# A scheduling edge between the down matmuls of one unit and the gate of the next

## The chip, the core and the metric

The kernel runs on one core of one Trainium2 chip. Its time is the device time of one execution in microseconds (us), and the median of three runs of the kernel before is 2629.54 us (2627.05 to 2629.81). Engines are named as in the profile: PE is the matmul engine, PEld its weight loads, ACT the activation engine, DVE the vector engine, POOL the general-purpose engine, SP the queue that issues the DMAs.

## What is computed

A batch of 8 sequences of 3008 rows with 256 features goes through a spectral layer (a real FFT along the sequence, a complex 256x256 product with a bias, soft thresholding at 0.01, the inverse FFT) and then, row by row, through a feed-forward layer:

```python
X = np.fft.rfft(x, axis=1)
Yr = Xr @ w_r - Xi @ w_i + b_r
Yi = Xr @ w_i + Xi @ w_r + b_i
Yr = np.sign(Yr) * np.maximum(np.abs(Yr) - lam, 0.0)      # Yi the same
y = np.fft.irfft(Y, n=x.shape[1], axis=1)
...
h = x @ w_in                       # 256 -> 2048
g = h * np.clip(h + 3.0, 0.0, 6.0) / 6.0
return (g @ w_out).astype(np.float32)     # 2048 -> 256
```

The change touches only the order of the feed-forward part.

## The kernel before

The 24064 rows are cut into 47 chunks of 512. The hidden width of 2048 is cut into 8 bands of 256, so there are 47 x 8 = 376 **units**, a chunk and a band each. A unit has three parts.

**The up product** (`block`, through the helper at L137) is 7 **groups** of three matmuls, 256 columns wide, a Strassen-like scheme on high and low parts of the numbers. Their numbers are the `n` of `block(i, n, ...)`. One PSUM tile `pb` collects groups 1, 6, 7 and 4 one upon the other, and after each of them ACT copies the sum out (`p1`, `u2`, `u3` at L585, and the last one straight into `h` at L619) before the next group may add to it. The next group can't begin before that copy has been read out. The same holds when the tile changes hands: `pb` has two buffers, so group 1 of unit i+2 waits for the `h` copy after group 4 of unit i. I call the four places (1 to 6, 6 to 7, 7 to 4, and 4 to group 1 of unit i+2) the **hand-overs** of `pb`. A tile `pc` with one buffer takes groups 5 and 3, a tile `pd` with one buffer group 2; DVE adds them to the copies (L590) and so fills `h`.

**The gate** (`gate`) is four operations in a row on the whole unit, 128x1024: `r = relu(h + 3)` on ACT (L626), `r = min(r, 6) * h` on DVE (L628), the high part `gs` by a cast on ACT (L130), the low part `gs` by a subtraction on DVE (L131). ACT and DVE carry out their instructions strictly in the order of the program.

**The down product** (`down`) is 12 matmuls of 512 columns (L649) into two PSUM tiles `po`: eight that need the high part of `gs` and four that need its low part. After the eighth band of a chunk `po` is scaled (`ot`) and stored.

The spectral layer of the later sequences is laid between the units: `fill` calls its generators by a table of slots. It brings matmuls into `ps_a`, copies, casts and DMAs, and it comes to an end before the units do, so that the last units stand almost alone.

The Python code only gives the instructions and their data. The order on each engine is made by a list scheduler, which walks a modelled timeline: of the instructions whose inputs are there it takes the one that comes first in the code, and `tc.high_priority()` lifts the copies and adds of the up product. So the down matmuls of a unit go wherever the model has both parts of `gs` ready and PE free. In the code, `gate(i-1)` begins in pass i of the loop and `down(i-3, step)` is spread over the same pass; the code's order therefore already has the first operation of gate i+1 ahead of the downs of unit i.

Of the kernel before, what the change touches and what calls it, by code (L numbers as in the profile page):

```python
# [13 lines left out]
AF = mybir.ActivationFunctionType  # L14
# [86 lines left out]
def spectral_ffn(ctx: ExitStack, tc: tile.TileContext, x, w_r, w_i, bias, w_in, w_out, f47, f64, g64, sgn, out):  # L101
    nc = tc.nc
# [11 lines left out]
    def space(shape, dt, name, tag=None):  # L114
        tag = tag or name
        return sb.tile(shape, dt, name=name, tag=tag, bufs=depth.get(tag, 1))
# [11 lines left out]
    def split(hi, lo, src, on=None):  # L128

        nc.scalar.copy(out=hi, in_=src)  # L130
        (on or nc.vector).tensor_tensor(out=lo, in0=src, in1=hi.bitcast(F32), op=ALU.subtract)  # L131
# [14 lines left out]
    def loaded(src, rows, cols, name, at=None):  # L146

        hi = const.tile([rows, cols], F32R, name=name + "_hi")
        lo = const.tile([rows, cols], F32R, name=name + "_lo")
        st = const.tile([rows, cols], F32, name=name + "_all") if at is None else at  # L150
        nc.sync.dma_start(out=st[:rows, :cols], in_=src)
        return hi, lo, st[:rows, :cols]
# [5 lines left out]
    nf = NFT // 2  # L158
    three = const.tile([P, 1], F32, name="three")
# [192 lines left out]
    with tc.issue_after(stores[-1].ins):  # L352
        r, k = [loaded(w, P, 2 * D, n, t) for w, n, t in ((w_r, "w_r", spare[7]), (w_i, "w_i", spare[8]))]
# [219 lines left out]
            yield  # L573

    units = [(c, f) for c in range(NC) for f in range(nf)]
    hs, ps_of, keep, gs, pos = {}, {}, {}, {}, {}

    def block(i, n, ps, start):
        c, f = units[i]
# [42 lines left out]
    def gate(i):  # L622

        h = hs.pop(i)
        r = space([P, 2, T], F32, "r")
        nc.scalar.activation(out=r, in_=h, func=AF.Relu, bias=three, scale=1.0)  # L626
        yield
        nc.vector.scalar_tensor_tensor(out=r, in0=r, scalar=6.0, in1=h, op0=ALU.min, op1=ALU.mult)  # L628
        t = gs[i] = space([P, 2, 2, T], F32R, "gs")
        split(t[:, 0], t[:, 1], r)  # L630
        yield
# [6 lines left out]
    )  # L638

    def down(i, step):  # L640

        c, f = units[i]
        g = gs[i]
        for u, dh, which, low in STEPS[step]:
            if f == 0 and step < 2 and u == 0 and which == "l":
                pos[dh] = ps_o.tile([P, 512], F32, name=f"po{dh}")
            ft = 2 * f + u
            w = wout_s["hl".index(which)]
            nc.tensor.matmul(  # L649
                out=pos[dh],  # L650
                lhsT=w[:, ft * D + dh * P : ft * D + (dh + 1) * P],
                rhs=g[:, low, u],
                start=f == 0 and u == 0 and which == "l",
                stop=f == nf - 1 and u == 1 and low == 1,
            )
            if f == nf - 1 and u == 1 and low == 1:
                ot = space([P, T], F32, "ot")
                if dh:
                    nc.vector.tensor_scalar(out=ot, in0=pos[dh], scalar1=1.0 / 6.0, scalar2=None, op0=ALU.mult)
                else:  # L660
                    nc.scalar.mul(out=ot, in_=pos[dh], mul=1.0 / 6.0)
                nc.sync.dma_start(out=out[dh * P : (dh + 1) * P, c * T : (c + 1) * T], in_=ot)
# [68 lines left out]
    for i in range(n + 3):  # L731
        for kind, f in ((in_band, i), (out_band, i - 3)):
            while 0 <= f < nf and (kind, f) not in ready:
                turn(LATE)
        if i < n:
            phase_a(i)
        gated(i - 2)
        fill(4 * i)
        if 0 <= i - 3 < n:
            down(i - 3, 0)  # L740
        if 0 <= i - 1 < n:
            phase_c(i - 1)
        fill(4 * i + 1)
        if 0 <= i - 3 < n:
            down(i - 3, 1)
        if i < n:
            phase_b(i)
        fill(4 * i + 2)
        if 0 <= i - 3 < n:
            down(i - 3, 2)  # L750
        if 0 <= i - 1 < n:
            phase_d(i - 1)
            gates[i - 1] = gate(i - 1)
            gated(i - 1)
        fill(4 * i + 3)
        if 0 <= i - 3 < n:
            down(i - 3, 3)
            gs.pop(i - 3)
# [47 lines left out]
```

## Time and profile before

| | |
|---|---|
| median of three runs | 2629.54 us |
| the profiled execution | 2630.53 us |
| its span, first to last instruction | 2628.8 us |
| PE busy | 2554.0 us (97%), 16392 matmuls |
| DVE busy | 1967.7 us (75%) |
| ACT busy | 1816.7 us (69%) |
| POOL busy | 762.9 us (29%) |
| mean granted clock of the matmul engine | 0.993 |
| unit 16 begins | 263.2 us |
| unit 325 begins | 2338.2 us |

Times in the rows are us from the first instruction, and a row's second number is how long the instruction (or the merged run of xN of them) took. Matmuls overlap in the records: one of 256 columns is listed with 0.28 us, yet the next starts 0.115 us later. What PE does is therefore read from starts, not from lengths. A bracket `[0.46 <-ACT p L585]` says that the engine was idle for 0.46 us before that instruction, and what released it.

### The profile page before, as it was taken

How to read it: one execution, taken by the hardware profiler on the slowest of the kernel's cores; microseconds unless marked ns; L12 is line 12 of the kernel's file. 1: busy time of each engine (PE TensorE's matmuls, PEld its weight loads, DVE VectorE, ACT ScalarE, POOL GpSimd, SP SyncE). 2: the span in 40 equal slices, each digit the busy share in tenths (PEclk: the TensorE clock that was granted, in tenths of full speed). 3: DMA queues.
4: the chain of work that ended last, by engine and by line, in shares of the span. 5: the costliest groups of instructions: out<-in, count | busy, mean ns of one | idle time of the engine just before them, and what ended most of it. 6: DMA issues, size and time to landing. Idle time of an engine off the chain costs nothing.

```text
span 2628.8 us, 44438 instructions
## 1 busy us (share of the span) xinstructions
PE 2554.0 (97%) x16392; PEld 2278.1 (87%) x16392; DVE 1967.7 (75%) x3195; ACT 1816.7 (69%) x3578; POOL 762.9 (29%) x726
## 2 busy tenths in 40 slices
PE   5789999999999999999999999999999999999999
PEld 4568989988898988998898888898989889888887
DVE  7777877777777777777778777787777777666766
ACT  5467776767677676676766677766776766776666
POOL 3223333333323332333314243233321121131310
PEclk8999999999999999999999999999999999999999
DMA  8643422232123212322223222222222111110000
GB/s 245 204 127 91 121 83 79 82 89 69 56 85 90 76 58 64 86 86 82 62 66 91 75 65 74 74 81 80 66 76 64 44 60 50 40 31 25 12 17 17
DMA packets 150081, 199.97 MB, mean 76 GB/s; under 512 B 16847, under 2 KB 103943, under 8 KB 149863
## 3 DMA queue, kind: packets, MB, share of 16 engines
q1 hardware_dynamic: 149863, 197.13, 25.7%
q8 instruction: 129, 2.11, 0.4%
q14 instruction: 89, 0.73, 0.1%
HBM read 97.45 MB, written 74.97 MB: 66 GB/s over the span
## 4 chain that ended last, share of the span: by engine, by line
PE 83%; DVE 6%; ACT 5%; DMA 4%; issue 1%; SPq 0%; POOL 0%; ACTq 0%; DVEq 0%
PE po L649 37%; PE pb L137 17%; PE ps_a L137 10%; PE pc L137 9%; PE pd L137 4%; PE ps_a L523 3%; PE ps_a L394 2%; ACT r L626 2%; DVE r L628 1%; ACT gs L130 1%; DMA scr<-a 1%; DMA xin<-in_x 1%; DVE gs L131 1%; DVE h L590 1%; DMA zt<-tc 1%
## 5 line engine op out<-in xcount | busy, mean ns | idle before, releaser
L649 PE MATMUL po<-gs,w_out_hi 128*128 128x512 f32 x3008 | 1008.5, 396 | 0.0
L628 DVE SCALAR_TENSOR_TENSOR r<-r,h 128x1024 f32<-128x1024 f32 x376 | 485.2, 1290 | 253.0 <-ACT r L626 250.9
L649 PEld LDWEIGHTS po<-gs,w_out_hi 128*128 128x128 f32 x3008 | 540.6, 188 | 83.7
L649 PE MATMUL po<-gs,w_out_lo 128*128 128x512 f32 x1504 | 602.9, 401 | 5.3 <-ACT gs L130 3.2
L137 PE MATMUL pb<-yb,w_in_hi 128*128 128x256 f32 x3008 | 570.1, 279 | 0.0
L626 ACT ACTIVATE r<-h,three 128x1024 f32<-128x1024 f32 x376 | 435.6, 1158 | 193.8 <-DVE h L590 191.1
L131 DVE TENSOR_TENSOR gs<-r,gs 128x1024 fp32r<-128x1024 f32 x376 | 481.9, 1282 | 75.6 <-ACT gs L130 74.1
L137 PEld LDWEIGHTS pb<-yb,w_in_hi 128*128 128x128 f32 x3008 | 459.1, 188 | 18.2
L130 ACT CAST gs<-r 128x1024 fp32r<-128x1024 f32 x376 | 396.7, 1055 | 97.3 <-DVE r L628 94.5
L590 DVE TENSOR_TENSOR h<-pc,u 128x256 f32<-128x256 f32 x752 | 315.3, 419 | 183.7 <-PE pc L137 168.4
L131 POOL TENSOR_TENSOR yb<-T,yb 128x256 fp32r<-128x256 f32 x184 | 176.7, 966 | 908.5 <-ACT yb L130 905.3
L137 PE MATMUL pb<-yb,w_in_lo 128*128 128x256 f32 x1504 | 430.5, 287 | 3.8 <-ACT p L585 0.9
L585 ACT COPY u<-pb 128x256 f32<-128x256 f32 x752 | 279.4, 374 | 112.6 <-PE pb L137 93.8
L649 PEld LDWEIGHTS po<-gs,w_out_lo 128*128 128x128 f32 x1504 | 282.7, 188 | 63.8 <-ACT gs L130 14.3
L137 PEld LDWEIGHTS pb<-yb,w_in_lo 128*128 128x128 f32 x1504 | 282.6, 188 | 28.2 <-ACT h L619 4.0
L137 PE MATMUL pc<-yb,w_in_hi 128*128 128x256 f32 x1504 | 296.8, 279 | 0.0
L137 PEld LDWEIGHTS pc<-yb,w_in_hi 128*128 128x128 f32 x1504 | 229.8, 188 | 11.7
L137 PE MATMUL pc<-yb,w_in_lo 128*128 128x256 f32 x752 | 217.7, 289 | 2.0 <-DVE h L590 1.7
L585 ACT COPY p<-pb 128x256 f32<-128x256 f32 x376 | 140.3, 374 | 71.6 <-PE pb L137 70.5
L619 ACT COPY h<-pb 128x256 f32<-128x256 f32 x376 | 141.2, 376 | 53.0 <-PE pb L137 51.7
L590 DVE TENSOR_TENSOR h<-pd,p 128x256 f32<-128x256 f32 x376 | 157.0, 418 | 19.8 <-ACT p L585 13.5
L137 PEld LDWEIGHTS pc<-yb,w_in_lo 128*128 128x128 f32 x752 | 141.6, 188 | 16.4 <-DVE h L590 3.9
(139 smaller groups left out, 3873.7 us busy)
## 6 DMA issues: line engine op xcount, KB each, us to landing
bt<-scr SPq DMA_DIRECT2D x96, 256.0 KB, 3.0
scr<-pt SPq DMA_DIRECT2D x96, 256.0 KB, 2.3
zt<-tc SPq DMA_DIRECT2D x376, 64.0 KB, 2.0
out<-ot SPq DMA_DIRECT2D x94, 256.0 KB, 2.3
scr<-a SPq DMA_DIRECT2D x96, 240.0 KB, 2.6
qt<-scr SPq DMA_DIRECT2D x96, 240.0 KB, 3.5
xin<-in_x SPq DMA_DIRECT2D x42, 480.0 KB, 4.6
f<-in_f SPq DMA_DIRECT2D x96, 128.0 KB, 2.7
```

The costliest lines, as they stand in the source:

```text
L130: nc.scalar.copy(out=hi, in_=src)
L131: (on or nc.vector).tensor_tensor(out=lo, in0=src, in1=hi.bitcast(F32), op=ALU.subtract)
L137: nc.tensor.matmul(out=ps, lhsT=a, rhs=b, start=start and n == 0, stop=stop and n == len(todo) - 1, skip_group_check=more,)
L394: nc.tensor.matmul(out=psv[:, dh, :, u, :], lhsT=data[:, u, dh * P : (dh + 1) * P], rhs=f[:, u, :], start=True, stop=True,)
L523: nc.tensor.matmul(out=ps[:, cs * w + g * rows : cs * w + (g + 1) * rows], lhsT=qt[:rows, cs, g, dh * P : (dh + 1) * P], rhs=f47_s[2][:row ...
L585: nc.scalar.copy(out=t, in_=ps)
L590: nc.vector.tensor_tensor(out=to, in0=ps, in1=keep.pop((i, n)), op=ALU.add)
L619: nc.scalar.copy(out=hs[i][:, 1, :H], in_=pb)
L626: nc.scalar.activation(out=r, in_=h, func=AF.Relu, bias=three, scale=1.0)
L628: nc.vector.scalar_tensor_tensor(out=r, in0=r, scalar=6.0, in1=h, op0=ALU.min, op1=ALU.mult)
L649: nc.tensor.matmul(out=pos[dh], lhsT=w[:, ft * D + dh * P : ft * D + (dh + 1) * P], rhs=g[:, low, u], start=f == 0 and u == 0 and which == ...
```

## The change

Two helpers are added. `gated_by` remembers the first gate operation of each unit, and `ordered` hands the scheduler a dependency of a kind that emits no semaphore: it binds the order that the scheduler makes, not the running engines. From unit 16 on every down matmul of unit i gets such an edge from the ACT operation `r = relu(h + 3)` of unit i+1. The instructions are the same ones.

```diff
-        nc.scalar.activation(out=r, in_=h, func=AF.Relu, bias=three, scale=1.0)
+        gated_by[i] = nc.scalar.activation(out=r, in_=h, func=AF.Relu, bias=three, scale=1.0)
...
+    def ordered(later, earlier):
+        why = mybir.DependencyInfo(mybir.DependencyClass.NoSync, mybir.DependencyReason.DATA)
+        tc.add_manual_dep(later.ins, earlier.ins.name, why, reason="order")
...
-            nc.tensor.matmul(
+            made_by = nc.tensor.matmul(
                 out=pos[dh],
...
+            if i + 1 in gated_by and i >= 2 * nf:
+                ordered(made_by, gated_by[i + 1])
```

What that does to the order, counted over units 16 to 375 in the two built programs (the PE work that stands between the last matmul of the one and the first of the other, at the pace of the matmuls in the trace before):

| on PE | before | now |
|---|---|---|
| hand-overs of `pb` with no group between | 1 | 21 |
| with one group of three (0.35 us) between | 24 | 78 |
| with two groups (0.70 us) between | 23 | 157 |
| with more | 1390 | 1182 |
| least work between the last group of a unit's `h` and its first down matmul, units 20 to 371 | 3.25 us | 6.16 us |
| least work between groups 5 and 3 of `pc`, same units | 0.35 us | 2.32 us |
| waits of down matmuls for a semaphore, whole program | 779 | 51 |

The first place is on PE, near the end, around units 369 to 371 (`pb_29635`, `pb_29688` and `pb_29747` are the `pb` of units 369, 370 and 371; `yb_29486` is the operand of group 4, `yb_29368` that of group 1, `yb_29451` that of group 5, `yb_29510` that of group 3, `yb_29333` that of group 2; `gs_29701` and `gs_29648` are the gates of units 368 and 367). Before:

```order
L137 MATMUL pb_29635<-yb_29486,w_in_lo_79 128x256 [waits Activation_49]
L137 MATMUL pb_29635<-yb_29486,w_in_hi_78 128x256 x2
L137 MATMUL pd_29748<-yb_29333,w_in_lo_79 128x256 [waits DVE_49]
L137 MATMUL pd_29748<-yb_29333,w_in_hi_78 128x256 x2
L137 MATMUL pc_29707<-yb_29510,w_in_lo_79 128x256 [waits DVE_49]
L137 MATMUL pc_29707<-yb_29510,w_in_hi_78 128x256 x2
L649 MATMUL po0_29763<-gs_29701,w_out_lo_227 128x512 [waits Activation_49]
L649 MATMUL po0_29763<-gs_29701,w_out_hi_226 128x512
...
L137 MATMUL pb_29688<-yb_29427,w_in_lo_79 128x256 [waits Activation_49]
L137 MATMUL pb_29688<-yb_29427,w_in_hi_78 128x256 x2
L137 MATMUL pb_29747<-yb_29368,w_in_lo_79 128x256 [waits Activation_49]
L137 MATMUL pb_29747<-yb_29368,w_in_hi_78 128x256 x2
```

Now, the same place:

```order
L137 MATMUL pb_29688<-yb_29392,w_in_lo_79 128x256 [waits Activation_49]
L137 MATMUL pb_29688<-yb_29392,w_in_hi_78 128x256 x2
L137 MATMUL pb_29635<-yb_29486,w_in_lo_79 128x256 [waits Activation_49]
L137 MATMUL pb_29635<-yb_29486,w_in_hi_78 128x256 x2
L137 MATMUL pb_29747<-yb_29368,w_in_lo_79 128x256 [waits Activation_49]
L137 MATMUL pb_29747<-yb_29368,w_in_hi_78 128x256 x2
L137 MATMUL pd_29748<-yb_29333,w_in_lo_79 128x256 [waits DVE_49]
L137 MATMUL pd_29748<-yb_29333,w_in_hi_78 128x256 x2
L137 MATMUL pc_29707<-yb_29451,w_in_lo_79 128x256 [waits DVE_49]
L137 MATMUL pc_29707<-yb_29451,w_in_hi_78 128x256 x2
L653 MATMUL po0_29310<-gs_29648,w_out_lo_227 128x512
L653 MATMUL po0_29310<-gs_29648,w_out_hi_226 128x512
```

Group 1 of unit 371 stood behind groups 2 and 3, eight down matmuls and one more group; now it stands right behind group 4 of unit 369, whose copy it waits for. The down matmuls, of a unit one earlier than before, carry no wait of their own any more and stand twelve in a row.

The second place is on ACT, the same units (`r_29736` and `r_29797` are the gates of units 369 and 370, `h_29690` is the `h` of unit 370; `u2_29784`, `u3_29775` and `p1_29811` are copies out of `pb`). Before:

```order
L619 COPY h_29637<-pb_29635 128x256 [waits PE_49]
L626 ACTIVATE r_29736<-h_29637,three_75 128x1024 [waits DVE_49,Activation_49]
L585 COPY u3_29775<-pb_29688 128x256 [waits PE_49]
L585 COPY p1_29756<-pb_29747 128x256 [waits PE_49]
L130 CAST gs_29760<-r_29736 128x1024 [waits DVE_49]
L619 COPY h_29690<-pb_29688 128x256 [waits PE_49]
L585 COPY u2_29784<-pb_29747 128x256 [waits PE_49]
L626 ACTIVATE r_29797<-h_29690,three_75 128x1024 [waits DVE_49,Activation_49]
```

Now:

```order
L130 CAST gs_29701<-r_29683 128x1024 [waits DVE_49]
L667 ACTIVATE ot_29740<-po0_29310 128x512 [waits DMAHW6_49,DMAHW5_49,PE_49]
L585 COPY u3_29775<-pb_29688 128x256 [waits PE_49,Activation_49]
L619 COPY h_29690<-pb_29688 128x256 [waits PE_49]
L585 COPY u2_29784<-pb_29747 128x256 [waits DVE_49]
L626 ACTIVATE r_29736<-h_29637,three_75 128x1024 [waits Activation_49]
L585 COPY p1_29811<-pb_29802 128x256 [waits PE_49]
L130 CAST gs_29760<-r_29736 128x1024 [waits DVE_49]
```

The gate of unit 369 stood ahead of the copies `u3` and `h` of unit 370 and of `u2` of unit 371; now it stands behind all three. The wait for DVE, which the gate had, is now on the copy `u2` right ahead of it: `u2` has two buffers, and this copy overwrites the one that DVE's last add to the `h` of unit 369 has to read first.

## Rows read from the trace of the kernel before

**Rows 1.** The head of the page: the span, and busy time, share and instructions of each engine.

```profile
span 2628.8 us, 44438 instructions
PE 2554.0 (97%) x16392; PEld 2278.1 (87%) x16392; DVE 1967.7 (75%) x3195; ACT 1816.7 (69%) x3578; POOL 762.9 (29%) x726
```

**Rows 2.** Busy time by stretch. The columns are the stretch, its length, then the busy us (and instructions) of PE, PEld, DVE, ACT and POOL, the granted clock as a share of 2.4 GHz, the share of the DMA engines and GB/s. The stretches begin with units 16, 100, 200, 325 and (after 2338.2) run to unit 370.

```profile
263.20:845.60 582.40, 577.97 (x3764) 521.67 (x3764) 445.43 (x709) 413.03 (x825) 194.59 (x176) 1.00 0.29 82
845.60:1519.50 673.90, 669.60 (x4342) 602.33 (x4341) 509.14 (x832) 472.78 (x942) 218.91 (x196) 1.00 0.26 75
1519.50:2186.70 667.20, 663.25 (x4331) 598.80 (x4330) 509.46 (x836) 468.38 (x927) 183.56 (x177) 1.00 0.24 70
2338.20:2582.90 244.70, 244.07 (x1541) 218.18 (x1540) 167.90 (x258) 170.04 (x325) 54.82 (x60) 1.00 0.05 17
```

**Rows 3.** PE in order of time, one unit near the end (start, us, what): two groups, four down matmuls, five groups, eight down matmuls.

```profile
2598.66 0.28 PE L137 MATMUL pb<-yb,w_in_lo 128*128 128x256 f32 x1
...
2599.01 0.28 PE L137 MATMUL pb<-yb,w_in_lo 128*128 128x256 f32 x1
...
2599.37 1.09 PE L649 MATMUL po<-gs,w_out_hi 128*128 128x512 f32 x4
2600.29 0.28 PE L137 MATMUL pc<-yb,w_in_lo 128*128 128x256 f32 x1
...
2603.92 0.28 PE L137 MATMUL pb<-yb,w_in_lo 128*128 128x256 f32 x1
```

**Rows 4.** The costliest groups of instructions, the seven of the gate and of the copies and adds (line, engine, operation, out<-in, shapes, count | busy us, mean ns of one | idle us before them, and what ended most of it).

```profile
L628 DVE SCALAR_TENSOR_TENSOR r<-r,h 128x1024 f32<-128x1024 f32 x376 | 485.2, 1290 | 253.0 <-ACT r L626 250.9
L626 ACT ACTIVATE r<-h,three 128x1024 f32<-128x1024 f32 x376 | 435.6, 1158 | 193.8 <-DVE h L590 191.1
L131 DVE TENSOR_TENSOR gs<-r,gs 128x1024 fp32r<-128x1024 f32 x376 | 481.9, 1282 | 75.6 <-ACT gs L130 74.1
L130 ACT CAST gs<-r 128x1024 fp32r<-128x1024 f32 x376 | 396.7, 1055 | 97.3 <-DVE r L628 94.5
L590 DVE TENSOR_TENSOR h<-pc,u 128x256 f32<-128x256 f32 x752 | 315.3, 419 | 183.7 <-PE pc L137 168.4
L585 ACT COPY u<-pb 128x256 f32<-128x256 f32 x752 | 279.4, 374 | 112.6 <-PE pb L137 93.8
```

**Rows 5.** The waits of the weight loads: who waited for whom, us in total, times, longest.

```profile
PEld po L649 <- ACT gs L130: 14.3, 44, 1.3
PEld pb L137 <- ACT h L619: 4.0, 15, 0.3
PEld pc L137 <- DVE h L590: 3.9, 10, 0.7
```

**Rows 6.** PE in order of time: down matmuls that had to wait for `gs`, the first (unit 37), one of the middle (unit 201, the longest) with the matmuls ahead of it, and the last (unit 375).

```profile
436.92 0.46 PE L649 MATMUL po<-gs,w_out_lo 128*128 128x512 f32 x1
...
1544.71 0.40 PE L137 MATMUL pb<-yb,w_in_hi 128*128 128x256 f32 x2
1546.23 0.51 PE L649 MATMUL po<-gs,w_out_lo 128*128 128x512 f32 x1 [1.12 <-ACT gs L130]
...
2621.45 0.50 PE L649 MATMUL po<-gs,w_out_lo 128*128 128x512 f32 x1 [0.68 <-ACT gs L130]
```

**Rows 7.** PE in order of time: the first and the last time that group 3 of `pc` waited for the add that reads group 5.

```profile
436.49 0.36 PE L137 MATMUL pc<-yb,w_in_lo 128*128 128x256 f32 x1
...
2616.74 0.38 PE L137 MATMUL pc<-yb,w_in_lo 128*128 128x256 f32 x1 [0.44 <-DVE h L590]
```

**Rows 8.** The only hand-over of `pb` with no group between (unit 32): PE and ACT in order of time.

```profile
381.36 0.40 PE L137 MATMUL pb<-yb,w_in_hi 128*128 128x256 f32 x2
...
381.80 0.37 ACT L585 COPY p<-pb 128x256 f32<-128x256 f32 x1
...
382.22 0.38 PE L137 MATMUL pb<-yb,w_in_lo 128*128 128x256 f32 x1 [0.46 <-ACT p L585]
...
382.45 0.40 PE L137 MATMUL pb<-yb,w_in_hi 128*128 128x256 f32 x2
```

**Rows 9.** A hand-over from group 4 to group 1 of unit i+2 with one group between: the last one of its kind (unit 362), ACT and PE in order of time.

```profile
2548.20 0.38 ACT L619 COPY h<-pb 128x256 f32<-128x256 f32 x1 [0.27 <-PE pb L137]
2548.21 0.40 PE L137 MATMUL pb<-yb,w_in_hi 128*128 128x256 f32 x2
...
2548.63 0.38 PE L137 MATMUL pb<-yb,w_in_lo 128*128 128x256 f32 x1
...
2548.85 0.40 PE L137 MATMUL pb<-yb,w_in_hi 128*128 128x256 f32 x2
```

**Rows 10.** The chain of waits of the stretch 2595 to 2605, in order of time (start, us, what): one turn from gate to gate.

```profile
2598.08 1.17 ACT r L626
...
2599.27 1.24 DVE r L628
...
2600.53 1.06 ACT gs L130
...
2601.62 1.23 DVE gs L131
2602.85 0.35 DVE h L590
...
2603.28 1.16 ACT r L626
```

More of the change, by code (lines that the diff above doesn't have):

```diff
@@ L575, in spectral_ffn @@
     units = [(c, f) for c in range(NC) for f in range(nf)]
-    hs, ps_of, keep, gs, pos = {}, {}, {}, {}, {}
+    hs, ps_of, keep, gs, pos, gated_by = {}, {}, {}, {}, {}, {}
     def block(i, n, ps, start):
```

## The prediction

> **What bounds the kernel now.** I read the head of the page first: PE is busy 2554.0 us of 2628.8, no other engine over 75% [rows 1]. Then the busy time by stretch: from unit 16 on PE is never idle for long (577.97 of 582.40 us, 244.07 of 244.70 towards the end) and its clock is granted in full [rows 2]. PE's order is the one that counts, and a reordering can win or lose only what PE spends waiting. To size that I went to PE's starts. In the unit of [rows 3] a group of three takes 0.35 us (2598.66 to 2599.01), four downs 0.92 us (2599.37 to 2600.29) and the whole unit, 7 groups and 12 downs, 5.26 us (2598.66 to 2603.92): seven times 0.35 plus twelve times 0.23 is 5.2, so nothing is lost there. Where a start comes later than this pace allows, PE waited. The waits of the weight loads give the main reasons: the downs wait for the cast half of `gs`, 14.3 us in 44 waits, more than all else from unit 16 on [rows 5].
>
> The second thing to see is the loop from gate to gate, which passes over ACT and DVE: relu, product, cast, subtraction, the last add into the next `h`, the next relu. In the late stretch it takes 5.20 us (2598.08 to 2603.28) [rows 10], hardly less than PE's 5.26. Earlier, PE also has the spectral matmuls and takes about 6.7 us for a unit (673.90 us for units 100 to 199 [rows 2]); there the loop has room.
>
> **The change part by part.** Nothing is added or removed; only places move. The durations are those of the profiled execution, 2630.5 us with what lies around its span, 1.0 above the median of the runs. Before unit 16 nothing changes.
>
> *What goes, first:* the downs' waits for `gs`. Counting from starts, with the slower restart behind each wait, 63 units lose 19.1 us at their first down, from 0.07 us at 436.92 to 0.95 us at 2621.45, the longest 1.4 us at 1546.23 [rows 6]. The last two, 1.6 us, belong to the drain of the kernel, where the downs of units 374 and 375 wait whatever the order. The order now has at least 6.16 us of PE work between a unit's `h` and its downs, where it had 3.25 to 5.6 in most of the cases that waited. The gate's four operations sum to 1.16 + 1.29 + 1.06 + 1.28 = 4.8 us [rows 4]; the first downs need only the first three, 3.5 us, and the queues of ACT and DVE took the rest of the old distance. At 6.16 I take the wait to be gone: -17.5 us.
>
> *What goes, second:* group 3 of `pc` waiting for DVE's add of group 5. 31 such waits lose 6.1 us, the first 0.08 us at 436.49, the last 0.71 us at 2616.74 [rows 7]. The last stays, being in the drain. The distance rises from a least of 0.35 us to a least of 2.32 us; a few of the old waits came at larger ones, so -5 us.
>
> *What comes, first:* hand-overs of `pb` with nothing between. In the one case of before, group 1's last pair starts at 381.36, the copy at 381.80, and group 6 only at 382.22; its second matmul follows 0.23 us later instead of 0.12 [rows 8]. Against the pace that is 0.73 us. There are 20 more of these: +14.6 us.
>
> *Second:* hand-overs with one group between. Before, 24 of them wait 0.31 us on average. Of the kind from group 4 to the next unit's group 1 there are twelve, 0.35 us on average, the first at 484.11, the last at 2548.63: that copy starts at 2548.20 and takes 0.38 us, and group 1 starts as it ends [rows 9]. The copy alone cannot be hidden by one group. There are 54 more; at 0.34 us, +18.4 us.
>
> *Third:* hand-overs with two groups between, 134 more. Of the 23 before only two waited, 0.02 us a piece over all: +2.7 us. This is the soft spot: 0.70 us is just the length of copy plus signals, so an ACT that is busy with a relu (1.16) or a cast (1.06 us) [rows 4] would turn each into a wait. If a third of a microsecond fell on each, it would be +40 us.
>
> *Fourth:* the one `pc` buffer is now taken again sooner after group 3 (31 places at two groups' distance, at 0.05 us before for the same distance): +1.7 us.
>
> *The gate that moves on ACT:* at the places shown, the relu is now behind a `u2` copy that itself waits for the add that the relu needs. So that copy, 0.37 us [rows 4], lies inside the loop instead of in its shadow: 5.20 + 0.37 = 5.57 us in the late units, above PE's 5.26. I don't add it: it is the same lateness seen from ACT that the short hand-overs show on PE, and over the 50 units from 325 on, whose PE takes 244.70 us for the first 45 of them, 5.4 a unit [rows 2], it would be 50 x (5.57 - 5.4) = 8 us or, against 5.26, 15 us. The hand-overs of those units alone count 15 with nothing and 14 more with one group between, 15 x 0.73 + 14 x 0.34 = 16 us. The two views agree.
>
> Sum: -17.5 - 5 + 14.6 + 18.4 + 2.7 + 1.7 = +14.9 us, of which the middle of the kernel makes about nothing and the units from 325 on nearly all. 2630.5 + 14.9 - 1.0 = 2644 us.
>
> Bounds. Below: if short hand-overs cost only the idle time shown, 0.46 us for none between [rows 8] and 0.2 for one, the costs are 20 x 0.46 + 54 x 0.2 = 20 us, and with -22.5 the sum is -2.5; if PE's other small waits of the middle, some 8 us, went as well, -10. Above: the third item at +40 gives +52. I take the middle values because they are means of what the same distance cost before.
>
> **The rivals.**
> *Faster.* Two short hand-overs often follow each other on PE (group 1 of one unit and group 4 of another). While PE waits for the first copy, ACT comes round to the second, and only one of the two is paid. With half of the one-group cases free and the rest as above the costs are 14.6 + 9 = 24 us; with the waits of two-group cases at nothing and 8 us of other waits gone, the sum is -22.5 + 24 - 8 = -6, 2623 us. For it: two hand-overs in a row at 2548.63 and after, where the second was nearly free. Against it: the late units had almost no waits to give back. It decides if the hand-overs' mean price falls below 0.3 us.
>
> *Much slower.* The loop, not the hand-over, sets the late units: with the `u2` copy (0.37) and, where DVE now has an add (0.42) [rows 4] between the subtraction and the last add, 5.20 + 0.37 + 0.42 = 6.0 us. 50 units x (6.0 - 5.4) = 30 us instead of 16, and the same lateness of ACT makes some of the two-group cases in the middle wait, 91 x 0.15 = 14 us: 2644 + 14 + 14 = 2672 us at the end of it, 2660 in between. For it: the new ACT order. Against it: the add comes between in only some of those units.
>
> *No change.* The middle gains a little more (5 us), the end loses a little less (8 us): 2631 us. For it: gains and costs are each over 20 us and nearly cancel in the middle.
>
> *The clock.* More frequent short waits on PE could cost the granted clock. No row speaks for it: the stretch with the 1.4 us wait kept 1.00 [rows 2, 6]. The Trainium skill's page "TensorE: Matmul & The Clock Gate", section "A second HAM failure mode: psum-queue depth-cycling", says that frequent short idling between groups of matmuls, while PSUM tiles are cycled, can make the clock swing between its two levels. By that rule the late units, with a wait in nearly every unit, would run partly at the lower level; if a tenth of the 290 us from unit 325 on ran at half speed, 15 us would come on top, 2659 us. The trace of before, with about one wait in three units, doesn't agree.
>
> **How the numbers follow.** The forecast, +5 to +22, 2635 to 2652 us: 0.42. Much slower (2652 to 2675): 0.20. No change (2624 to 2635): 0.18. Faster (under 2624): 0.17. The clock: 0.03. What a measurement of this kernel can tell from no change is about 0.2%, 5 us. So slower 0.42 + 0.20 + 0.03 = 0.65, same 0.18, faster 0.17. The range leaves out some 0.1 at either end: 2621 to 2664.
>
> **What would show it.** The downs' waits for ACT's cast should fall from 14.3 us to under 3; weight loads of `pb` waiting for `h` (4.0 us now [rows 5]) and for `p` should grow to 20 us or more. Unit 16 to 325 should take the same time within 8 us (2075 us now), and the end from unit 325 on some 15 us more. I am wrong if the middle gets clearly shorter, if hand-overs with nothing between cost under 0.4 us, or if the end takes no longer.

## The result, and the profile after

The changed kernel takes 2665.11 us (median of 4 runs, 2663.78 to 2666.64) against 2629.68 us of the kernel before, a ratio of 1.014 with an interval of 1.0128 to 1.0152. It is slower by 35 us, where +14.4 was forecast; the time lies 13 us above the forecast band (2635 to 2652) and just above the end of the wide range (2621 to 2664). The profiled execution took 2663.78 us, 33.3 more than that of before.

The head of the page after:

```profile
span 2662.0 us, 44624 instructions
PE 2579.6 (97%) x16392; PEld 2291.5 (86%) x16392; DVE 1958.8 (74%) x3195; ACT 1818.9 (68%) x3578; POOL 750.1 (28%) x726
```

The same matmuls, and 25.6 us more of PE "busy" than in [rows 1]: a wait shows in part as busy time, since a matmul behind one is listed as longer (0.39 us at 2442.61 further down, 0.28 at 2440.75, where nothing waits). DVE, ACT and POOL have no more work than before. So the time is in waits, and the place shows in the busy time by stretch (columns as in [rows 2]; first the stretches of units 16 to 99, 100 to 199, 200 to 299 and 325 to 369, then the two halves, units 16 to 299 and unit 300 to PE's last start):

```profile
263.83:848.11 584.28, 579.72 (x3771) 521.90 (x3769) 440.23 (x710) 413.07 (x827) 191.36 (x176) 1.00 0.29 82
848.11:1520.35 672.24, 668.69 (x4331) 601.57 (x4329) 503.79 (x831) 473.63 (x938) 206.39 (x195) 1.00 0.26 75
1520.35:2185.37 665.02, 662.25 (x4304) 597.47 (x4303) 501.01 (x832) 467.08 (x925) 183.29 (x177) 1.00 0.24 69
2342.09:2606.70 264.61, 255.71 (x1548) 222.43 (x1548) 171.13 (x258) 171.22 (x325) 57.83 (x60) 1.00 0.05 15
...
263.83:2185.37 1921.54, 1910.67 (x12400) 1720.94 (x12399) 1445.04 (x2371) 1353.78 (x2688) 581.04 (x547) 1.00 0.26 75
2185.37:2657.36 471.99, 456.29 (x2780) 398.18 (x2778) 311.15 (x478) 303.27 (x570) 87.70 (x93) 1.00 0.07 23
```

The two halves of the kernel before, which stand in none of the groups ahead:

```profile
263.16:2186.72 1923.56, 1910.88 (x12436) 1722.85 (x12435) 1464.08 (x2377) 1354.21 (x2692) 597.10 (x547) 1.00 0.26 76
2186.72:2624.12 437.40, 434.92 (x2743) 388.40 (x2742) 302.41 (x473) 299.97 (x566) 86.27 (x93) 1.00 0.08 24
```

Units 16 to 299 take 1921.5 us for 1923.6; the units from 300 on take 472.0 for 437.4. The two parts don't hold the same work, though: the new order leaves 37 more matmuls behind the start of unit 300 (x2780 for x2743), the twelve downs of one unit among them. At the pace of the rows (0.117 us for 256 columns, 0.233 for 512) they take about 5.6 us, an estimate. At equal work the middle loses some 3.5 us and the end some 29. Nearly all of the loss is at the end, and the clock is granted in full (1.00) there.

The waits of the weight loads, the lines that answer to [rows 5] (who waited for whom: us, times, longest):

```profile
PEld pb L137 <- ACT h L619: 19.4, 37, 0.8
PEld pc L137 <- DVE h L590: 11.8, 24, 0.8
PEld pb L137 <- ACT p L585: 9.0, 34, 0.8
PEld pb L137 <- ACT u L585: 7.3, 23, 1.1
...
PEld po L653 <- ACT gs L130: 2.4, 1, 2.4
```

The downs' wait for the cast went from 14.3 us in 44 waits to one wait in the drain. In its place the groups wait for ACT's copies out of `pb` and, not foreseen at that size, for DVE's add that frees `pc` (3.9 before, 11.8 now).

For the whole account I use one measure below. It is the time from the start of the matmul ahead to the start of a group's (or the downs') first matmul, less the median of that difference for the same two widths; where the second matmul behind a wait starts late too, that is added. Each wait is put down to the buffer or the operand that became ready last. From unit 16 on, in us:

| wait of | before | after | difference | forecast |
|---|---|---|---|---|
| downs for `gs` | 19.5 | 5.5 | -14.0 | -17.5 |
| group 3 for `pc` | 6.3 | 0.8 | -5.5 | -5 |
| hand-overs of `pb`, none between (1, then 21) | 0.7 | 15.3 | +14.6 | +14.6 |
| one group between (24, 78) | 7.5 | 18.6 | +11.1 | +18.4 |
| two groups between (23, 157) | 0.6 | 9.1 | +8.5 | +2.7 |
| more between | 2.0 | 6.2 | +4.2 | 0 |
| group 5 of the next unit for `pc` | 0.7 | 16.3 | +15.6 | +1.7 |
| group 2 for `pd` | 2.6 | 3.8 | +1.2 | 0 |
| sum | 39.8 | 75.6 | +35.7 | +14.9 |

(The sums are of unrounded terms.) The chain of waits after, two turns of a late unit (start, us, what), where [rows 10] had relu, product, cast, subtraction, add and relu:

```profile
2569.69 1.13 DVE gs L131
2570.82 0.34 DVE h L590
...
2571.21 0.62 PE pc L137 x3
2571.83 2.80 PE po L653 x12
2574.63 0.34 PE pd L137 x3
...
2576.49 0.38 ACT h L619
...
2576.91 0.62 PE pb L137 x3
2577.53 0.34 PE pc L137 x3
2577.88 2.79 PE po L653 x12
...
2581.53 1.13 DVE gs L131
2582.66 0.34 DVE h L590
```

The chain goes through PE now, the twelve downs in a row (2.80 us) among it, and the turns shown pass over a copy or over a subtraction with an add right behind it. From downs to downs it is 6.05 us (2571.83 to 2577.88), where the unit of [rows 3] took 5.26.

### The profile page after: what moved, and what is told of

Read it like the earlier page. It is cut to its first block, busy times and chain, and to the rows that moved or that the text cites. A ratio compares the mean times of both kernels' runs of the same rounds, so it can differ in the third digit from the quotient of the medians.

```text
span 2662.0 us, 44624 instructions
## 1 busy us (share of the span) xinstructions
PE 2579.6 (97%) x16392; PEld 2291.5 (86%) x16392; DVE 1958.8 (74%) x3195; ACT 1818.9 (68%) x3578; POOL 750.1 (28%) x726
## 4 chain that ended last, share of the span: by engine, by line
PE 86%; DVE 6%; ACT 4%; DMA 2%; issue 1%; POOL 0%; SPq 0%; DVEq 0%; ACTq 0%; POOLq 0%
PE po L653 37%; PE pb L137 19%; PE ps_a L137 11%; PE pc L137 9%; PE pd L137 5%; PE ps_a L523 3%; PE ps_a L394 3%; DVE gs L131 1%; DVE r L628 1%; DVE h L590 1%; DMA xin<-in_x 1%; ACT gs L130 1%; ACT r L626 1%; DMA scr<-a 1%; ACT h L619 1%
## 5 line engine op out<-in xcount | busy, mean ns | idle before, releaser
L653 PE MATMUL po<-gs,w_out_hi 128*128 128x512 f32 x3008 | 954.2, 395 | 0.0
L653 PEld LDWEIGHTS po<-gs,w_out_hi 128*128 128x128 f32 x3008 | 561.6, 188 | 104.8
L653 PE MATMUL po<-gs,w_out_lo 128*128 128x512 f32 x1504 | 592.7, 394 | 2.0 <-ACT gs L130 2.0
L131 DVE TENSOR_TENSOR gs<-r,gs 128x1024 fp32r<-128x1024 f32 x376 | 475.9, 1266 | 145.0 <-ACT gs L130 143.2
L137 PE MATMUL pb<-yb,w_in_hi 128*128 128x256 f32 x3008 | 578.5, 279 | 0.0
L137 PE MATMUL pb<-yb,w_in_lo 128*128 128x256 f32 x1504 | 449.4, 300 | 17.7 <-ACT h L619 11.2
L131 POOL TENSOR_TENSOR yb<-T,yb 128x256 fp32r<-128x256 f32 x184 | 168.3, 922 | 958.4 <-ACT yb L130 937.3
L137 PEld LDWEIGHTS pc<-yb,w_in_hi 128*128 128x128 f32 x1504 | 243.2, 188 | 20.6
L131 POOL TENSOR_TENSOR yb<-raw,yb 128x256 fp32r<-128x256 f32 x138 | 138.9, 1011 | 62.7 <-ACT yb L130 62.6
```

Of the source, the lines that this page charges most:

```text
L137: nc.tensor.matmul(out=ps, lhsT=a, rhs=b, start=start and n == 0, stop=stop and n == len(todo) - 1, skip_group_check=more,)
L653: made_by = nc.tensor.matmul(out=pos[dh], lhsT=w[:, ft * D + dh * P : ft * D + (dh + 1) * P], rhs=g[:, low, u], start=f == 0 and u == 0 an ...
```

## The experiments

The theories: **short hand-overs** (A, where an expectation uses letters): each place where a group follows too soon on the copy or add it needs pays its own price, and the total is the sum over places. **The loop** (B), later **lateness**: the later the downs of a unit stand, the longer the turn from gate to gate. **Clumping**: twelve downs in a row cover no hand-over, and all seven groups crowd into the rest. In the table the counts are hand-overs of `pb` with 0/1/2 groups between, the waits are by the measure above. The last column is from the one profiled execution and holds shifts of work like the one told above (2739 to 2802 matmuls behind the start of unit 300, by kernel); where a reading hangs on that, the text says so.

| kernel | us | ratio (interval) | counts | all waits | group 5 for `pc` | units 16 to 299, from 300 |
|---|---|---|---|---|---|---|
| before | 2629.7 | 1 | 1/24/23 | 39.8 | 0.7 | 1923.6, 437.4 |
| changed | 2665.1 | 1.014 (1.0128 to 1.0152) | 21/78/157 | 75.6 | 16.3 | 1921.5, 472.0 |
| edge up to unit 299 | 2634.5 | 1.0023 (1.0014 to 1.0033) | 4/57/92 | 44.6 | 7.4 | 1921.3, 441.4 |
| edge from unit 300 | 2658.2 | 1.0115 (1.01 to 1.013) | 19/43/93 | 69.6 | 8.2 | 1920.9, 466.3 |
| low downs alone | 2599.8 | 0.9893 (0.9879 to 0.9908) | 0/5/17 | 18.7 | 2.4 | 1894.7, 434.1 |
| add of `p1` put back | 2652.2 | 1.0091 (1.0074 to 1.0108) | 7/88/160 | 65.2 | 15.7 | 1921.9, 461.2 |
| late, but split | 2621.9 | 0.9969 (0.9959 to 0.998) | 1/38/49 | 37.3 | 8.3 | 1908.3, 442.9 |
| edge on eight downs | 2599.1 | 0.9885 (0.9869 to 0.9902) | 0/1/20 | 15.4 | 2.8 | 1894.3, 434.6 |
| low behind product | 2639.6 | 1.0039 (1.0024 to 1.0054) | 3/56/101 | 48.0 | 9.7 | 1918.2, 450.0 |
| low alone, behind product | 2609.4 | 0.9925 (0.991 to 0.994) | 0/0/34 | 24.1 | 2.8 | 1901.8, 438.8 |
| clumped, not late | 2622.1 | 0.9972 (0.9961 to 0.9983) | 3/17/43 | 38.2 | 1.7 | 1913.6, 438.2 |
| changed, `pc` twice | 2693.6 | 1.0244 (1.0228 to 1.0259) | 0/54/80 | 64.2 | 16.2 | 1970.6, 455.9 |
| before, `pc` twice | 2715.1 | 1.0329 (1.0313 to 1.0345) | 0/18/27 | 80.5 | 8.1 | 1997.7, 449.1 |
| add ahead of subtraction | 2622.6 | 0.9974 (0.9964 to 0.9984) | 0/4/80 | 33.7 | 5.3 | 1910.9, 440.1 |

The diffs below are against the changed kernel where nothing else is said.

**Where it comes from: the edge up to unit 299, and from unit 300 on.**

```diff
-            if i + 1 in gated_by and i >= 2 * nf:
+            if i + 1 in gated_by and 2 * nf <= i < 300:
...
-            if i + 1 in gated_by and i >= 2 * nf:
+            if i + 1 in gated_by and i >= 300:
```

> The edge only for units 16 to 299; from unit 300 on the order is as in the kernel before. Theory A (the short hand-overs of pb between PE and ACT are the cost, each at its own price, wherever it stands): 57 hand-overs with at most one group between remain in units 16 to 299 against 21 before, 13 us more, less the 15 us of down waits that go: 2625 to 2633 us. Theory B (a loop through the downs, PE to DVE to PE, sets the late units, where PE has no spectral work to fill): units 16 to 299 last as long as before within 5 us, and so does the end: 2627 to 2636 us. A cost that is spread over all units instead: 2640 us or more.

> The edge only from unit 300 on. Theory A: 18 hand-overs with nothing and 23 with one group between, 18 x 0.73 + 23 x 0.25 = 19 us, less 4 us of down waits: 2645 us. Theory B: the late units take 5.85 us each as in the changed kernel, the whole loss of 29 to 33 us comes back: 2657 to 2665 us.

Against their own runs of before the parts cost 6 us and 30 us, together the whole. Both times fall into the ranges of the loop, and neither into those of short hand-overs (2634.5 against 2633 at most; 2658.2 against 2645): those sums had no term for hand-overs with two groups between, nor for the wait for `pc` (8.2 us in the second kernel). Units 16 to 299 and the last 76 have 104 more hand-overs each with two groups or less between (42 to 146, and 6 to 110), yet at equal work the former lose some 3.5 us in the changed kernel and the latter 29. In the middle the downs' waits that go pay for most of the new ones; at the end there were few to give back (5 of the 19.5 us). The first kernel's 441.4 us at the end are the shift of work (its order has 2780 matmuls there too), not a loss.

**The edge on the four low downs alone.**

```diff
-            if i + 1 in gated_by and i >= 2 * nf:
+            if i + 1 in gated_by and i >= 2 * nf and low:
```

> The edge only for the four downs of each unit that read the low part of gs; the eight of the high part are free. Hand-overs of pb with nothing or one group between fall to 5 (25 before, 99 in the changed kernel); groups 5 and 3 of pc stand at least 0.93 us apart (0.35 before); downs stand somewhat later behind their h (least 4.1 against 3.5 us in units 16 to 299). Theory A: 6 us of hand-overs, 5 us of pc waits and some 8 of the 19 us of down waits go: 2608 to 2620 us. Theory B: in the late units no pd group with its add stands between the cast and the subtraction more often than before, so they stay at 5.45 us; the middle gains as in A: 2610 to 2625 us. If it is not faster than 2624, the down waits were not what the order can give back.

Faster than both kernels, and by more than either theory said. The two halves of this kernel:

```profile
263.25:2157.95 1894.70, 1890.04 (x12426) 1713.82 (x12425) 1454.71 (x2376) 1361.44 (x2691) 574.76 (x547) 1.00 0.27 77
2157.95:2592.03 434.08, 431.18 (x2753) 386.26 (x2752) 303.46 (x474) 304.48 (x566) 87.69 (x93) 1.00 0.07 24
```

The middle gains 29 us on before. Of 39.8 us of waits 18.7 are left, the downs' at 9.4 and the hand-overs' at 3.7: the high downs, though without an edge, come a little later too (at the median 6.68 us of PE work after `h` in units 16 to 299, for 6.14), and the two parts still stand apart with groups between. The waits account for 21 of the 32 us that both halves gain in the profile; what gives the rest is not shown.

**Is it DVE's add inside the loop?** The add of `p1` had come between subtraction and last add in late units. Here it is ordered behind the add of `u2` two units back (`add_by` holds every add by its unit and copy).

```diff
-            nc.vector.tensor_tensor(out=to, in0=ps, in1=keep.pop((i, n)), op=ALU.add)
+            made_by = add_by[i, n] = nc.vector.tensor_tensor(out=to, in0=ps, in1=keep.pop((i, n)), op=ALU.add)
+        if n == "p1" and i >= 2 * nf + 3:
+            ordered(made_by, add_by[i - 2, "u2"])
```

> The changed kernel, and one more edge without a semaphore: DVE's add of pd into h of unit i comes behind its last add into h of unit i-2. In the late units it then stands behind the subtraction of the low part and the last add, not ahead of them. Hand-overs from unit 300 on: 7 with nothing, 26 with one group between (17 and 25 in the changed kernel). Theory A: 10 x 0.73 = 7 us less: 2656 to 2660 us. Theory B: the piece downs, pd group, add is out of the loop, the late units (75 from 300 on) fall from 5.87 to about 5.55 us: 2635 to 2648 us.

2652 lies between the two, some 4 us from either. The add is out of the chain and units from 300 on still take 461 us, 24 more than before with the same amount of work (in the changed kernel it was 29 at equal work). Of the 13 us gained 10 are the hand-overs with nothing between, of which 14 went with the new order. So the add is not what makes the late units slow, or only a small part of it.

**Late, but split.** High downs as changed, low ones later still, so that the twelve no longer stand together.

```diff
-                ordered(made_by, gated_by[i + 1])
+                ordered(made_by, (prod_by if low else gated_by)[i + 1])
```

(`prod_by` holds the cast of the unit's gate.)

> The eight downs of the high part stay behind relu of the next unit, the four of the low part are put later still, behind the cast of the next unit: every down is as late as in the changed kernel or later, but the order now has the twelve downs of a unit in two stretches, eight and four, with groups between. Hand-overs of pb with 0/1/2 groups between: 1/38/49 instead of 21/78/157 (units from 300 on: 1/13/15). Theory of short hand-overs (each pays its own price: 0.73, 0.24, 0.06 us): they cost 12.8 us instead of 49, about 2630 us. Theory of clumping (twelve downs in a row leave all seven groups of a unit, with their copies and adds, to one short stretch): the late loss goes, units from 300 on take 430 to 445 us instead of 472, 2615 to 2635 us. Theory of lateness (the later the downs of a unit come, the longer the loop from them through the last adds to the next gate): 2655 to 2680 us, units from 300 on 465 us or more.

Lateness falls: the first downs stand as far behind `h` as in the changed kernel (from unit 300 on 7.0 us of PE work at the median in both), and the late loss is down from 34.6 to 5.5 us (at equal work from 29 to about 2). Clumping and short hand-overs both allow it; the time is inside the range of the one and 8 us under the other.

**The first four downs free, the other eight behind the relu.**

```diff
-            if i + 1 in gated_by and i >= 2 * nf:
+            if i + 1 in gated_by and i >= 2 * nf and (low or u):
```

> The first four downs of a unit (the high part, first half of the columns) are free, the other eight come behind relu of the next unit. Hand-overs with 0/1/2 groups between: 0/1/20 (the kernel with the edge on the four low downs alone: 0/5/17; it took 2599.8 us). Theory of short hand-overs: 1.5 us for them, and the downs that are let wait for the low half only where it is not there: 2596 to 2604 us. Theory of clumping: eight free-standing downs in two stretches of four leave groups between: 2594 to 2604 us. Theory of lateness: eight of twelve downs late costs two thirds of the loss of the changed kernel from unit 300 on (+20 us on 434): 2615 to 2640 us.

As good as the edge on four (the intervals lie on each other), and against lateness once more. These two are the best versions found.

**Two tests of clumping.** From the runs so far I made a price table: the mean wait of a hand-over by the PE work between. For `pb` it is 0.73, 0.26, 0.05 and 0.02 us with none, one, two and three groups. Three kernels were forecast by it. The first has the low downs behind the product of the next unit (`prod_by` holds the product here), one group between the parts. The second puts that edge on the low downs only (`and low`). The third has no edge to a gate at all; its downs come behind group 1 three units on (`last_of` holds the last matmul of a group), which puts twelve in a row at 76 places without being late:

```diff
-            if i + 1 in gated_by and i >= 2 * nf:
-                ordered(made_by, gated_by[i + 1])
+            if i >= 2 * nf and (i + 3, 1) in last_of:
+                ordered(made_by, last_of[i + 3, 1])
```

> The eight high downs behind relu of the next unit, as in the changed kernel, the four low ones behind the product of the next unit: as late as there, with one group between the two parts. A price table was made from the runs so far: mean wait of a hand-over by the PE work that lies between (pb: 0.73, 0.26, 0.05, 0.02 us; pc and downs likewise). Theory of short hand-overs: the table put on this kernel's order gives 47.6 us of waits from unit 16 on (39.8 measured before, 75.5 in the changed kernel), that is 2638 us, 2632 to 2645. Theory of lateness: 2655 us or more. Theory of clumping with one group between counting as clumped: 2650 us or more.

> The eight high downs free as in the kernel before, the four low ones behind the product of the next unit, one step later than in the kernel with the edge on the low downs alone (2599.8 us). Hand-overs of pb with 0/1/2 groups between: 0/0/34. Theory of short hand-overs: the price table gives 28.2 us of waits (25 to 28 us for the kernels at 2600, which had 15 to 19), that is 2600 to 2618 us. Theory of lateness: later low downs give some of the gain back, 2610 to 2630 us.

> No edge to the next unit's gate: all twelve downs come behind the last matmul of group 1 three units on, one step later than in the kernel before. The order has 76 stretches of twelve downs in a row (10 in the kernel before, 139 in the changed kernel, 64 of these from unit 300 on), but hand-overs of pb with 0/1/2 groups between are few: 3/17/43 (1/24/23 in the kernel before). Theory of short hand-overs: the price table gives 39.2 us of waits, 2625 to 2633 us. Theory of clumping by itself: 66 more stretches of twelve at 0.3 to 0.4 us each (29 us over 75 units from 300 on in the changed kernel) cost 20 to 26 us, 2648 to 2660 us.

All waits came to 48.0, 24.1 and 38.2 us where the table said 47.6, 28.2 and 39.2, and the first two times fall into its ranges; the third is 3 us under its own. (The second gives back 10 us of what the edge one step earlier had won; so far lateness has a point; in the first, where it asked for 2655 us or more, it fell.) The forecast of clumping, 2648 us or more, fell: 66 more stretches of twelve, and the kernel is 7 us faster than before. But that holds for the middle alone. Only 5 of these stretches belong to units from 300 on, where the changed kernel has 59, so this test says nothing on the late units; the kernel with `pc` twice below does. In these three kernels what counts is which groups stand close to the copy or add they need.

**What the table does not explain: `pc`.** Made without the changed kernel and its two halves, the table gives that kernel 60.5 us of waits instead of 75.6; 10.9 of the missing 15.1 are the wait of group 5 for `pc` (5.4 against 16.3). PE and DVE of the changed kernel in order of time around one of these waits:

```profile
2440.75 0.28 PE L137 MATMUL pc<-yb,w_in_lo 128*128 128x256 f32 x1
2440.87 0.39 PE L137 MATMUL pc<-yb,w_in_hi 128*128 128x256 f32 x2
...
2441.01 1.22 DVE L131 TENSOR_TENSOR gs<-r,gs 128x1024 fp32r<-128x1024 f32 x1
...
2441.89 0.39 PE L137 MATMUL pb<-yb,w_in_hi 128*128 128x256 f32 x2
2442.14 0.42 DVE L590 TENSOR_TENSOR h<-pc,u 128x256 f32<-128x256 f32 x1
...
2442.61 0.39 PE L137 MATMUL pc<-yb,w_in_lo 128*128 128x256 f32 x1 [0.34 <-DVE h L590]
...
2442.84 0.40 PE L137 MATMUL pc<-yb,w_in_hi 128*128 128x256 f32 x2
```

Group 3 (2440.75) is followed by three groups for `pb` and `pd`, then comes group 5. The add that frees `pc` could begin at about 2441.3, when group 3 has ended; but the subtraction of the gate is ahead of it in DVE's order and runs from 2441.01 for 1.22 us. The add begins at 2442.14, group 5 at 2442.61 instead of 2442.12, and its second matmul another 0.23 us later instead of 0.12: 0.60 us lost with three groups between. Of the 48 waits of this kind over 0.05 us, 37 with 13.8 us have the gate's subtraction directly ahead of the add and ending last. Before, the subtraction already stood somewhere ahead of this add in 303 of 359 units (directly ahead in 133), now it does in 347 (168). But from unit 300 on half of the places had 3.5 us of PE work or more between groups 3 and 5; now half have 1.05 us or less. So the queue cost next to nothing (0.7 us) while the distances were long; what the short distance costs without the queue is tested last.

**`pc` with two buffers**, in the changed kernel and, as its control, in the kernel before. To keep the number of PSUM tiles, the tile of the spectral matmuls gives one buffer up.

```diff
-    ps_a = ctx.enter_context(tc.tile_pool(name="ps_a", bufs=2, space=PSUM))
+    ps_a = ctx.enter_context(tc.tile_pool(name="ps_a", bufs=1, space=PSUM))
...
-        pc = ps_c.tile([P, 512], F32, name="pc")[:, :H]
+        pc = ps_c.tile([P, 512], F32, name="pc", bufs=2)[:, :H]
```

> The changed kernel with two buffers for pc (the projection's accumulator ps_a gives one up). No group waits for pc; the hand-overs of pb from unit 300 on are 0/44/26 with 0/1/2 groups between instead of 17/25/68. Theory of short hand-overs: the 16 us of waits for pc go, and from unit 300 on pb costs 12 us instead of 22; some 2622 to 2635 us where the projection with one buffer costs nothing (its control shows that), units from 300 on 440 to 450 us. Theory that the wait for pc is only where a longer loop through downs, adds and groups shows: the wait moves to another place, units from 300 on stay at 462 to 475 us.

> The kernel before with the same two buffers of pc and one of ps_a: the control. It had 6.3 us of waits of group 3 for pc and 0.6 of group 5. Theory of short hand-overs: 2622 to 2634 us, units from 300 on 434 to 438 us (437.4 before). If one buffer of ps_a costs something it shows in the units before 16 and in those up to 300.

The control is 85 us slower than the kernel before, 74 of them in units 16 to 299, where the spectral matmuls run. That the missing `ps_a` does it is the likely reading; it was not tried alone. Neither theory had it, so the absolute forecasts are void, and the pair has to be read against itself. Units from 300 on, first the changed kernel, then the control:

```profile
2232.62:2688.57 455.95, 450.15 (x2802) 397.23 (x2800) 314.06 (x488) 304.79 (x578) 93.07 (x96) 1.00 0.09 27
```

```profile
2258.65:2707.78 449.13, 439.76 (x2783) 391.81 (x2781) 312.55 (x481) 302.60 (x574) 91.85 (x94) 1.00 0.08 26
```

With two buffers the edge costs 6.8 us there (455.95 less 449.13) instead of 34.6, or some 4 at equal work (x2802 for x2783) instead of 29, and over the whole kernel it gains 21.5 us. The order still puts twelve downs in a row 63 times in the units from 300 on (59 in the changed kernel, 8 in the control), so clumping by itself is not what costs the late units their 29 us. In the units from 300 on the wait before group 5 is 1.4 us, where it was 8.5. That fits the wait for `pc` as a main part of the loss, but does not prove it alone: the order of `pb` changed too (no hand-over without a group between is left), and the wait before group 5 in the earlier units (14.8 us) is largely one for POOL's `yb`.

**The add ahead of the subtraction.** In the changed kernel, the add of `u2` of unit i+1 is put before the subtraction of unit i.

```diff
-        split(t[:, 0], t[:, 1], r)
+        nc.scalar.copy(out=t[:, 0], in_=r); (yield) if i + 1 < len(units) else None; sub_ = nc.vector.tensor_tensor(out=t[:, 1], in0=r, in1=t[:, 0].bitcast(F32), op=ALU.subtract); i >= 2 * nf and i + 1 in add_by and ordered(sub_, add_by[i + 1])
...
-            gated(i - 1)
+            gated(i - 1); gated(i - 2)
```

(`add_by` holds the last add into `h` of each unit.)

> The changed kernel, every down behind relu of the next unit as there, and on DVE the add of u2 (the one that reads pc after group 3 and frees it) of unit i+1 put ahead of the gate's subtraction of unit i, from unit 16 on. It stood behind the subtraction in 347 of 359 units. The order changes with it: hand-overs of pb with 0/1/2 groups between 0/4/80 instead of 21/78/157; the PE work between group 3 and the next group 5 stays as short as in the changed kernel (0.7 us at the quarter instead of 2.8 to 3.5 in the kernel before). Theory that pc waits because its add is queued behind the subtraction: the wait for pc falls from 16.2 to 2 to 5 us, waits in all 20 to 24 us, 2608 to 2616 us. Theory that the short distance alone sets it: the price table gives 15.4 us for pc and 33.9 in all, 2622 to 2628 us. Rival: the subtraction, now behind the add, is late for the low downs, waits for gs come back (14 us or more): 2625 us or more.

PE and DVE of this kernel around group 5 of the same unit as above:

```profile
2415.47 0.28 PE L137 MATMUL pc<-yb,w_in_lo 128*128 128x256 f32 x1
...
2416.01 0.42 DVE L590 TENSOR_TENSOR h<-pc,u 128x256 f32<-128x256 f32 x1 [1.99 <-PE pc L137]
...
2416.26 0.39 PE L137 MATMUL pb<-yb,w_in_hi 128*128 128x256 f32 x2
...
2416.35 1.22 DVE L630 TENSOR_TENSOR gs<-r,gs 128x1024 fp32r<-128x1024 f32 x1
...
2416.49 0.38 PE L137 MATMUL pc<-yb,w_in_lo 128*128 128x256 f32 x1
```

Only two groups between, the add comes as soon as group 3 is done, and group 5 starts when it is due (0.23 us after the pair of 2416.26). The wait for `pc` falls from 16.3 to 5.3 us, where the table without the queue said 15.4: on this point the queue is shown, as the distance from group 3 to group 5 stayed short. The time is 2622.6, in the range of the distance alone (2622 to 2628) and not 2608 to 2616, because other waits came: the downs' at 9.9, and hand-overs of `pb` with more than two groups between at 9.0 (6.2 in the changed kernel). The sum of all waits, 33.7, is what the table gives, by other terms. The kernel is 42 us faster than the changed one, of which 11 are group 5's wait for `pc` and 35 the hand-overs of `pb` (some others grew), so that its end (440 us from unit 300 on) can't be put down to the add alone. Nor are the downs where they were: of the 141 stretches of twelve 8 are left.

## Why the prediction was half right

**Right: the mechanism and the place.** The downs' waits went, short hand-overs came, the middle made little of it and the end paid. Units 16 to 324 were to take the same within 8 us: 2078.3 against 2075.1. That agrees partly by luck: some 30 matmuls, twenty of them downs, have moved behind the start of unit 325, about 6.0 us at the pace of the rows, and at equal work the middle loses some 9 us and the end 23. Hand-overs with nothing between cost 0.73 us each and 14.6 more in all, to the tenth. The weight loads of `pb` wait 28.4 us for `h` and `p`, where 20 or more was the sign. Group 3 for `pc` gave back 5.5 us, where 5 was expected.

**Wrong: "*Fourth*", the `pc` buffer taken again sooner.** It was put at +1.7 us, 31 places at 0.05, and measured +15.6: two thirds of the miss of 20.8 us. The step took its price from the same distance before and counted only places with two groups between. Distance alone did not set it: by the price table it makes 5.4 us, and with the add put ahead of the subtraction 16.3 us of waiting fell to 5.3. In most units (347 of 359) the add that frees `pc` stands in DVE's order behind a subtraction of 1.2 us, and before there was enough work on PE to hide both. The prediction named the cover for ACT's copies, but not for this add.

**Mis-sized: hand-overs of `pb` by distance.** One group between: +11.1 instead of +18.4, a mean of 0.24 us, not 0.34. Two groups: +8.5 instead of +2.7; more than two: +4.2 instead of nothing. The "soft spot" was real, at 0.06 us a place and not at the third of a microsecond of the upper bound; that ACT's relu and cast make it was not tested. All hand-overs together came to +38.4 against 35.7 forecast, so these errors nearly cancel, which is luck.

**Mis-sized: the downs.** 5.5 us of waits are left, not 2; the largest of them, 2.4 us, is unit 375's in the drain, where 1.6 had been left for two. Most of the rest are some 0.08 us each at downs whose `gs` had long been ready, and their cause is open.

**"The two views agree"** was the step that gave false comfort: 15 us for the end by the loop and 16 by the hand-overs. From unit 325 on the kernel takes 29.4 us more (315.3 for 285.9), 23 at equal work. Both views left out `pc` behind the subtraction (some 5.6 us of waits there) and the hand-overs with two groups between (some 4.5).

**The rivals.** *Much slower* had the number (6.0 us a turn; the changed kernel takes 5.8 to 5.9 in units 325 to 374), but not by its terms: with the DVE add taken out of the chain the late units keep most of their loss, and ACT's `u` copies, the other term, are 0.5% of the chain of waits from 2342 to 2657 us; the copy alone was not tested. *Faster* and *no change* fell with the time. The sign that *Faster* was to be decided by, a mean price below 0.3 us, did come for hand-overs with one group between (0.24), without the time that should follow. *The clock* fell too: 1.00 in every stretch from unit 16 on, also in the late units, which wait in nearly every turn. The Trainium skill's rule cited for it ("TensorE: Matmul & The Clock Gate", section "A second HAM failure mode: psum-queue depth-cycling") does not show here: the trace of the changed kernel keeps 1.00 from unit 16 to PE's last start, with these waits in it.

What stays open: why the two best kernels have 9 to 10 us less waiting than the price table gives them, most of it in the downs; which waits make the 11 us that the edge on the low downs gains beyond the account; and how the late loss divides between `pc` and the hand-overs of `pb`, since every edge that changed the one changed the other.

## What to carry to other kernels

A wait taken away by moving work can be paid for where that work was cover: list every buffer whose free distance shrinks, and price each by the queue of the engine that frees it, not by the distance alone. Ask of the freeing instruction what long one stands ahead of it in the same engine's order. And move no more than the gain needs, so that what is left still stands between the groups: here the same edge on four of the twelve downs turned a loss of 35 us into a gain of 29. And where two parts of a kernel are compared by a boundary in one engine's order, count the work on either side first: here 5.6 us of it had only changed sides.

## What was not expected of the hardware

Short waits in nearly every turn of the last units left the granted clock at 1.00, where the prediction gave a drop some chance. And one buffer less for the spectral tile, with one more for `pc`, went with 85 us, more than any order tried here.
